# A gated recurrence followed by a bilinear feed-forward layer: a new order of the first steps, and nine more matmuls of zeros

## The chip, the core and the metric

The kernel runs on one core of one Trainium2 chip. The core has five engines that run their own queues in order and wait for each other by semaphores: TensorE (PE, with its weight loads shown as PEld), VectorE (DVE), ScalarE (ACT), GpSimd (POOL) and SyncE (SP), of which GpSimd and SyncE here also issue the DMAs that load and store. TensorE writes only to PSUM, eight banks of 512 words in each of 128 partitions; VectorE and ScalarE read the results from there. The metric is the time of one execution on the device in microseconds (us). The profile adds the span from the first to the last recorded instruction, and the granted clock of TensorE, as a share of full speed.

## The reference

Two computations, one after the other. The first is a recurrence for each of 4 batches x 8 heads, over 768 positions with heads of 48. A state of 48 x 48 decays by a vector and takes up an outer product at each position, and a query reads it:

```python
for t in range(S):
    state = alpha[:, :, t, :, None] * state + np.einsum('bhd,bhe->bhde', k[:, :, t], v[:, :, t])
    y[:, :, t] = np.einsum('bhd,bhde->bhe', q[:, :, t], state)
```

The second takes y as 3072 tokens of 384 features (the 8 heads side by side) and computes `(x @ w_a) * (x @ w_b) @ w_out`, with w_a and w_b of 384 x 1536 and w_out of 1536 x 384.

## The kernel before

The recurrence is worked in chunks. A block holds 256 positions of two batches, so there are six blocks, numbered 0 to 5 (blocks 0 and 1 are the first 256 positions of batches 0, 1 and of 2, 3). Within a block each batch (called u, 0 or 1) is split into two chunks of 128 positions, called g, and into two halves of four heads, called a and b or h = 0 and 1. Logs of alpha are summed along a chunk by matmuls with a triangular matrix. The exponentials of these sums scale queries and keys, so that a chunk becomes: scores (keys times queries), masked to the past, times the values; plus the queries times the state carried into the chunk; and a state that is passed on. The feed-forward layer then takes a block's 512 tokens, 128 of the 1536 hidden features at a time (12 groups f): an a product, a b product, their product to SBUF, and from these the output with w_out.

The order of all instructions is written by hand in the string PROGRAM. Each entry names a block and then its steps; each step issues the instructions of one small function, and every engine runs its own in that order. The scheduler adds only the waits. A step stands in the queues of the engines that it uses, so moving it past steps of other engines changes nothing on its own.

The steps that the change touches, with their arguments and the lines of what they issue:

- ld (L547), W (L527), Wo (L530): loads of alpha, k, q, v for a block, columns lo to hi of w_a or w_b, and rows of w_out. The last letter names the issuing queue, P for GpSimd, Y for SyncE. W and Wo are on GpSimd.
- ln (L554): log of alpha on ScalarE. B u half bank (L589, L590): its running sums, in float32, for block 0, straight from the two logs of a pair of rows. l2 (L562), H, L, A2 (L636): the same for block 1, by sums of pairs, split in two parts.
- E u i and E u b (L665): the exponentials, of the negated and of the plain sums (their tile carries the name prod in block 0). mk and mq (L676): keys and queries times them, on VectorE. lv (L650): a correction of k or q for half of the rows.
- dk (L698) and de (L719): sums of logs over a chunk by matmuls with two columns, and their exponentials, which decay the state.
- C u h bank (L736): eight transposes of scaled keys and queries, and Ce (L958 or L960): their copy to SBUF.
- v (L769, L771) and vs (L958, L960): copies of the values, straight and with rows crossed.
- K u g bank (L792) or K2 (L805): the product of keys and values; k (L819, L822, L823): the next state from it.
- D u h bank (L837): scores. M (L846): masked by VectorE. Mc and Mm (L850, L854): copied by ScalarE and then masked.
- SB, SA (L866): the carried part of the output of u. Y (L866): the part from the scores. X (L902, L904): that output to SBUF, as the input x of the layer.
- a f u bank, b f u bank (L921): the gate products of group f, for u = 0, 1 or both (written *), with 256 or 512 columns in three matmuls. as (L927): the a product to SBUF, in one of three copies. pr (L935): a times b, on VectorE.
- o m half bank (L943), ot (L958, L960), st (L976): outputs of 128 tokens, their copy and their store.
- fill n bank (L572): n matmuls of a 128 x 128 by a 128 x 512 tile of zeros into a PSUM bank. Nobody reads the result.
- cm, c1, ci, cu, cus, cz, cs, c2, c3: constants and zeroed tiles.

A bank's new writer waits until its last result has been read. In the order before, TensorE's queue starts with fill 7, B 0b, B 0a, dk 0, C 0 1, fill 2, C 0 0, D 0 1, K 0 0, D 0 0, SB 0, B 1a, B 1b, dk 1, Y 0, SA 0, C 1 0, K 1 0, C 1 1, K 1 1, D 1 0 and then the first gate products: a 1, a 2, b 1, a 3 of u = 0, D 1 1, SB 1, b 3, b 2, b 0, a 0, b 4.

The fill step, the gate products and the copy of the a product are these lines:

```python
    def fill(n, i):
        for _ in range(n):
            nc.tensor.matmul(bank(i), lhsT=wz[:, :C], rhs=wz, start=True, stop=True)

    def ff(ch, w, f, us, i):
        n = len(range(B)[us]) * C
        ch.pf["ab"[w], f, us.start, us.stop] = p = bank(i)[:, :n]
        for kk in range(KT):
            nc.tensor.matmul(p, lhsT=(wa_t, wb_t)[w][:, kk, f * 128:(f + 1) * 128], rhs=ch.xT[:, kk, us, :], start=(kk == 0), stop=(kk == KT - 1))
```

Of the kernel before, what the change touches and what calls it, by code (L numbers as in the profile page):

```python
# [34 lines left out]
0: as 0 0; b 4 0 5  # L35
1: ln 0; l2 0 P
0: Mm 1 1 V; SA 1; Y 1; K 0 1 6; pr 2 0; a 4 0 0; as 4 0; b 5 0 7; k 1 1 V; a 5 0 4; X 1 V; a 1 1 2
0: a 2 1 0
1: ld q 1 P
0: a 3 1 1; pr 0 0; pr 4 0; b 1 1 3; Wo 0 6; k 0 1 V; as 5 0; a 4 1 4; b 3 1 5; b 4 1 6; as 1 1; a 0 1 2  # L40
1: ln 1; l2 1 P
0: pr 1 1
1: ra 0; lv 0 q P; ld k 1 P
0: a 5 1 3; pr 5 0; as 3 1; b 0 1 1; Wo 6 12; as 4 1; b 2 1 4; pr 3 1; a 10 * 5
1: H 1 V; L 1 V
0: a 11 * 7; as 0 1; as 2 1; pr 2 1
# [24 lines left out]
0: a 9 * 5; as 9 *; b 8 * 0
1: C 0 1 7; mq 1 V; Ce 0 1 V; C 0 0 2
0: b 9 * 1; pr 9 *; o 2 0 3; as 8 *; pr 8 *
1: Ce 0 0 S; D 0 0 4; Mc 0 0; K2 0 0 2 6
0: o 0 0 7; o 3 0 0
1: k 0 0 V; k 0 1 V; SB 0 4
3: ld a * P
1: mk 1 V; D 0 1 1; M 0 1
0: o 3 1 -; ot 3 V; st 3 Y
1: v 0 S; vs 0 0 S; vs 0 1 S; Mm 0 0 V; C 1 1 6; Ce 1 1 V  # L80
2: ln *
0: o 0 1 -; ot 0 S
# [24 lines left out]
1: b 10 0 6; pr 10 0; a 6 0 7; as 7 0; b 7 0 1; pr 7 0; b 5 0 5; as 5 0
2: lv 1 k P
1: b 11 0 6; pr 5 0; SA 1
2: mq 0 V  # L110
1: Y 1
2: mq 1 V
1: b 6 0 1
2: mk 1 V; E 0 i
1: as 6 0; a 0 0 0; b 0 0 7; pr 6 0; a 11 0 4; X 1 S; a 2 1 5; b 3 0 2; as 0 0; pr 0 0; as 11 0; a 3 0 3
1: as 3 0; a 8 0 4; b 9 0 0; b 2 1 1; a 6 1 3; pr 11 0; as 2 1; a 9 0 5; as 9 0; pr 3 0; o 2 0 2
# [1061 lines left out]
```

## Time and profile before

| what | value |
|---|---|
| timed runs | 189.12, 189.28, 190.45 us (median 189.28) |
| profiled execution | 190.44 us |
| its span | 188.7 us |
| TensorE busy | 181.9 us, 96% of the span |
| VectorE, ScalarE, GpSimd busy | 152.6, 120.1, 53.6 us |
| bytes read and written | 25.98 and 4.74 MB |
| mean granted clock of TensorE | 0.991 |

Busy time is the time in which an engine had an instruction under way. Matmuls are pipelined, so the rows of TensorE overlap: the time that one takes of the queue is read from its start to the start of the next. A row of the timeline gives its start, the time to the end of its last instruction, the engine, the line in the kernel, the operation, what it writes and reads, and how many instructions it merges; in brackets stands the idle time before it and what ended that. The rows of stretches give, for each engine, its busy time and the number of its instructions, then the granted clock and the DMA engines' share and rate. Granted clock that isn't recorded at the start of a trace is shown as full.

### The profile page before, as it was taken

Reading aid. Unit: us, or ns where it says so; the run is one execution under the profiler, and the core shown is the slowest. Engines: PE = TensorE matmul, PEld = TensorE weight load, DVE = VectorE, ACT = ScalarE, POOL = GpSimd, SP = SyncE. Lnnn points to the kernel's source line nnn. Section 1 sums busy time; section 2 is a strip of 40 time slices with the busy share of each in tenths; the row PEclk is TensorE's granted clock in tenths of the full one; section 3 lists DMA queues with packets and bytes.
Section 4 is the critical chain, followed back from the end, with each engine's and each line's share of the span. In section 5 each row is a group of like instructions: output and inputs, shape, how many; then the busy total and the mean of one; then the engine's idle time right before and its main releaser. Section 6 shows DMA issues by size and latency. Waiting matters only on the chain.

```text
span 188.7 us, 6347 instructions
## 1 busy us (share of the span) xinstructions
PE 181.9 (96%) x2693; PEld 122.3 (65%) x2709; DVE 152.6 (81%) x271; ACT 120.1 (64%) x228; POOL 53.6 (28%) x74
## 2 busy tenths in 40 slices
PE   7979999999999999999999999999999999999993
PEld 3969886566778886754445644555457477565992
DVE  2484889788979799998889899999999945696862
ACT  4364865579995797797697949965980451526230
POOL 8999654998062240003500003300000000000000
PEclk9987999999999999999999999999999999999999
DMA  5999999999999899989999699939500102110053
GB/s 125 263 225 195 261 235 254 230 231 257 247 214 129 129 215 276 275 237 182 198 173 271 144 116 167 112 107 165 89 0 9 43 0 83 44 43 0 0 170 127
DMA packets 66285, 29.43 MB, mean 156 GB/s; under 512 B 55776, under 2 KB 64624, under 8 KB 66256
## 3 DMA queue, kind: packets, MB, share of 16 engines
q1 hardware_dynamic: 47488, 16.34, 41.2%
q0 software_dynamic: 18624, 12.58, 39.3%
q8 instruction: 21, 0.34, 0.7%
q10 hardware_dynamic: 144, 0.10, 0.2%
q14 instruction: 8, 0.07, 0.1%
HBM read 25.98 MB, written 4.74 MB: 163 GB/s over the span
## 4 chain that ended last, share of the span: by engine, by line
PE 90%; ACT 6%; issue 2%; DVE 1%
PE psum L921 47%; PE psum L943 12%; PE psum L1032 11%; PE psum L866 5%; PE psum L837 3%; PE psum L589 2%; PE psum L590 2%; PE psum L736 2%; PE psum L572 2%; ACT vx L958 2%; PE psum L631 1%; ACT la L554 1%; PE psum L792 1%; PE psum L805 1%; PE psum L698 1%
## 5 line engine op out<-in xcount | busy, mean ns | idle before, releaser
L921 PE MATMUL psum<-xT,wb_t 128*128 128x512 bf16 (+1 forms) x263 | 55.8, 336 | 0.5 <-issue 0.2
L921 PE MATMUL psum<-xT,wa_t 128*128 128x512 bf16 (+1 forms) x262 | 55.2, 335 | 0.5 <-issue 0.2
L921 PEld LDWEIGHTS <-wa_t 128*128 128x128 bf16 x270 | 25.7, 98 | 19.2 <-issue 0.5
L921 PEld LDWEIGHTS <-wb_t 128*128 128x128 bf16 x270 | 25.5, 98 | 18.4 <-issue 0.5
L943 PE MATMUL psum<-wo_t,prod 128*128 128x384 bf16 x144 | 26.1, 327 | 0.0
L958 ACT ACTIVATE ot<-psum 128x384 f32<-128x384 f32 (+1 forms) x23 | 11.2, 487 | 17.7 <-PE psum L1032 15.4
L650 POOL TENSOR_TENSOR q_t<-q_t,ra 128x384 f32<-128x384 f32 x6 | 6.4, 1072 | 53.6 <-ACT ra L643 31.1
L943 PEld LDWEIGHTS <-prod 128*128 128x128 bf16 x144 | 13.3, 98 | 8.3
L958 ACT ACTIVATE vx<-v_t 32x384 bf16<-32x384 bf16 x26 | 13.5, 521 | 1.5 <-DVE vx L771 1.1
L1032 PEld LDWEIGHTS <-prod 128*128 128x128 bf16 x144 | 12.0, 98 | 1.2
L850 ACT ACTIVATE m<-psum 128x768 bf16<-128x768 f32 x14 | 11.0, 810 | 2.3 <-PE psum L837 2.3
L676 DVE TENSOR_TENSOR QKp<-q_t,beta 128x768 bf16<-128x768 f32 x10 | 9.4, 952 | 1.9 <-ACT beta L665 1.6
L554 ACT ACTIVATE la<-a_t 128x1536 f32<-128x1536 f32 (+2 forms) x9 | 9.5, 1054 | 1.7 <-DMA a_t<-in_alpha_dram 1.5
L676 DVE TENSOR_TENSOR QKp<-k_t,invb 128x768 bf16<-128x768 f32 x10 | 10.1, 1013 | 0.3
L846 DVE TENSOR_TENSOR m<-psum,mask 128x768 bf16<-128x768 f32 x10 | 9.5, 949 | 0.6 <-PE psum L837 0.6
L1044 DVE TENSOR_TENSOR ot<-psum,ot 128x384 f32<-128x384 f32 x9 | 5.0, 555 | 5.9 <-issue 3.2
L866 PE MATMUL psum<-m,vx 64*64 64x128 bf16 (+1 forms) x576 | 8.7, 205 | 0.0
L547 POOL DMA_DIRECT2D v_t<-in_v_dram x8 | 8.5, 1064 | 0.0
L866 PE MATMUL psum<-kqT,Sm 64*64 64x128 bf16 x144 | 7.5, 220 | 0.4 <-DVE Sm L819 0.4
L866 PEld LDWEIGHTS <-vx 64*64 64x64 bf16 x576 | 7.6, 108 | 0.1
L854 DVE TENSOR_TENSOR m<-m,mask 128x768 bf16<-128x768 bf16 x14 | 7.4, 550 | 0.0
L665 ACT ACTIVATE prod<-psum 128x384 f32<-128x384 f32 x8 | 3.5, 488 | 6.0 <-PE psum L590 6.0
(292 smaller groups left out, 361.5 us busy)
## 6 DMA issues: line engine op xcount, KB each, us to landing
out_dram<-ot SPq DMA_DIRECT2D x23, 192.0 KB, 2.7
q_t<-in_q_dram SPq DMA_DIRECT2D x3, 768.0 KB
k_t<-in_k_dram SPq DMA_DIRECT2D x3, 768.0 KB
a_t<-in_alpha_dram POOLq DMA_DIRECT2D x2, 768.0 KB, 11.7
v_t<-in_v_dram POOLq DMA_DIRECT2D x4, 384.0 KB, 7.6
a_t<-in_alpha_dram SPq DMA_DIRECT2D x2, 768.0 KB
a_t<-in_alpha_dram POOLq DMA_DIRECT2D x3, 384.0 KB, 7.5
k_t<-in_k_dram POOLq DMA_DIRECT2D x3, 384.0 KB, 7.3
```

The lines of the kernel that those rows point to most:

```text
L547: eng.dma_start(out=t[:, us, hs].rearrange("p b h r d -> p (b h) (r d)"), in_=src[ch.b0 + us.start:ch.b0 + us.stop, hs, ch.s * 2 * C:(ch.s ...
L554: nc.scalar.activation(out=ch.la[:, us, hs].rearrange("p b h r d -> p (b h r d)"), in_=ch.a[:, us, hs].rearrange("p b h r d -> p (b h r d) ...
L650: eng.tensor_mul(x, x, by)
L676: eng.tensor_mul(QKp[ch.c % 2][:, u, j, :, hs, :D], src[:, u, hs].rearrange("p h r d -> p r h d"), f)
L846: nc.vector.tensor_mul(m, x, maskn())
L850: nc.scalar.activation(out=m, in_=x, func=AF.Copy)
L854: eng.tensor_mul(m, m, maskn())
L866: nc.tensor.matmul(o, lhsT=lhsT, rhs=rhs, start=(g, c) not in begun, stop=False, skip_group_check=True)
L921: nc.tensor.matmul(p, lhsT=(wa_t, wb_t)[w][:, kk, f * 128:(f + 1) * 128], rhs=ch.xT[:, kk, us, :], start=(kk == 0), stop=(kk == KT - 1))
L943: nc.tensor.matmul(op, lhsT=ch.prod[:, f, at:at + C], rhs=wo_t[:, f, :], start=(f == 0), stop=(f == NFF - 1))
L958: nc.scalar.activation(out=o_, in_=i_, func=AF.Copy)
L1032: nc.tensor.matmul(o[:, g], lhsT=A[:, f, g * C:(g + 1) * C], rhs=W[:, f], start=(not more and (apart or g == 0) and f == 0), stop=(f == LH ...
```

## The change

The steps of blocks 0 and 1, up to block 1's first gate products, are written in a new order, with other PSUM banks. The same steps are there, with the same arguments apart from the banks. The one step whose count differs is fill: 7 and 2 before, and 7, 5, 2, 1, 2, 1 after. TensorE's queue now starts with fill 7, B 0b, B 0a, C 0 1, dk 0, fill 5, K 0 0, C 0 0, D 0 1, fill 2, SB 0, D 0 0, fill 1, dk 1, B 1a, B 1b, fill 2, C 1 0, Y 0, SA 0, fill 1, C 1 1, D 1 0, K 1 0, a 3, a 2, K 1 1, D 1 1, SB 1, a 0, a 1, b 2, b 3, b 1, SA 1, K 0 1, Y 1. On VectorE, Ce 0 1 stands ahead of mk 0a and mq 0a, M 0 1 ahead of M 0 0, mq 1a ahead of mk 1a and mq 1b ahead of mk 1b; in block 1, mq 1 and mk 1 stand ahead of M 0 1. On ScalarE, de 0 and v 0 change places, ln 1 stands ahead of vs 0 0, and E 1a b ahead of E 1a i. From block 2's transposes on, the listing is the same. The first lines of the diff, cut:

```diff
-0: E 0b i; mk 0b V; ld k 1 P; ld q 1 P; cm 1; W b 0 256; cz 0 v P; E 0b b; mq 0b V; ld v 1 P; W a 256 768; dk 0 2
-0: C 0 1 3; E 0a i; mk 0a V; cz 1 q P; E 0a b; mq 0a V; v 0 S; Ce 0 1 V; fill 2 0; W a 0 256; de 0; W b 256 512
-0: C 0 0 1; Ce 0 0 V; D 0 1 2; K 0 0 0; vs 0 0 S; W b 512 768; cs 1 m P
-1: ld a 0 P
-0: D 0 0 4; k 0 0 V; SB 0 0; M 0 0; ln 1; B 1a 6
-1: ld a 1 P
-0: W a 768 1536; c2 P; W b 768 1536; E 1a i; E 1a b; B 1b 4
-1: ld q 0 P
-0: dk 1 6
-1: ld k 0 P
-0: vs 0 1 V; E 1b i; M 0 1; Y 0; mk 1a V; mq 1a V; mk 1b V; SA 0; E 1b b; mq 1b V; C 1 0 7; Ce 1 0 V
-0: K 1 0 2; C 1 1 3; de 1; k 1 0 V; Ce 1 1 V
-1: ld v 0 P
-0: K 1 1 4; X 0 S; v 1 S; vs 1 1 V; D 1 0 0; Mc 1 0; a 1 0 5; vs 1 0 V; as 1 0; a 2 0 2; b 1 0 3; as 2 0
-0: a 3 0 0; pr 1 0; as 3 0; D 1 1 6; SB 1 1; Mm 1 0 V; b 3 0 5; Mc 1 1; b 2 0 0; b 0 0 3; pr 3 0; a 0 0 6
+0: E 0b i; mk 0b V; ld k 1 P; ld q 1 P; cm 1; E 0b b; mq 0b V; E 0a i; E 0a b; C 0 1 7; Ce 0 1 V; dk 0 4
+0: mk 0a V; de 0; fill 5 0; W b 0 256; mq 0a V; K 0 0 6; k 0 0 V; C 0 0 7; Ce 0 0 V; v 0 S; ln 1; D 0 1 0
+0: M 0 1; fill 2 2; SB 0 2; D 0 0 4; fill 1 6; dk 1 6; M 0 0; vs 0 0 S; B 1a 0; E 1a b; vs 0 1 V; E 1a i; mq 1a V; B 1b 4
+0: E 1b i; E 1b b; mk 1a V; fill 2 7; C 1 0 7; mq 1b V; cz 0 v P; ld v 1 P; W a 256 768; cz 1 q P; W a 0 256; Y 0; SA 0
+0: mk 1b V; fill 1 0; C 1 1 0; v 1 S; Ce 1 0 V; D 1 0 4; Ce 1 1 V; X 0 S; W b 256 512; vs 1 0 V; de 1; K 1 0 7; k 1 0 V
+0: a 3 0 1; W b 512 768; cs 1 m P; Mc 1 0; Mm 1 0 V; as 3 0; a 2 0 6; K 1 1 0
+1: ld a 0 P
+0: as 2 0; vs 1 1 V; D 1 1 2; Mc 1 1; SB 1 3; a 0 0 5; as 0 0; Mm 1 1 V; a 1 0 1; b 2 0 6; b 3 0 2; pr 3 0
+0: as 1 0; b 1 0 5; SA 1; K 0 1 7; Y 1; k 1 1 V; a 5 0 0; b 0 0 1; a 4 0 2; pr 2 0; b 4 0 6; X 1 V
...
```

The rest of block 0's gate products and of block 1 (its sums A2, transposes C, scores D and states K2, the outputs o of block 0, and block 1's first gate products) follow in the same manner:

```diff
-0: a 5 1 3; pr 5 0; as 3 1; b 0 1 1; Wo 6 12; as 4 1; b 2 1 4; pr 3 1; a 10 * 5
...
-0: b 5 1 0; b 10 * 2
...
-0: pr 0 1; b 6 * 1
...
-1: H 0 V; L 0 V; lv 1 q P; A2 0 3; lv 1 k P
-0: a 8 * 6; pr 5 1; pr 10 *
...
-1: C 0 1 7; mq 1 V; Ce 0 1 V; C 0 0 2
+0: pr 0 0; b 5 0 3; as 5 0; b 3 1 4; a 5 1 0
...
+1: ld v 1 P; A2 0 5; H 1 V
...
+0: pr 0 1; a 11 * 4; a 10 * 6; as 2 1; b 2 1 7; pr 2 1
...
+0: a 7 * 2; as 7 *; as 4 1; b 4 1 0; b 10 * 1; pr 4 1
+1: dk * 7; A2 1 2
...
+1: mq 0 V; mk 0 V
+0: b 9 * 7
+1: v 0 S; E 1 i; C 0 0 2
```

More of the change, by code (lines that the diff above doesn't have):

```diff
@@ L108 @@
[L108 to L116, printed above, removed]
+0: cz 1 v P
+1: Mc 0 0; vs 0 0 S
+0: o 3 0 6; o 0 0 1
+1: M 0 1; SB 0 2; vs 0 1 S
+0: o 3 1 -
+1: C 1 0 4; C 1 1 5; k 0 1 V; Mm 0 0 V; Ce 1 0 S
+2: ln *
+0: ot 3 V; o 0 1 -
+1: Ce 1 1 V; v 1 V; vs 1 1 V
@@ new lines @@
+0: st 3 Y
+2: l2s 0 V
+1: D 1 1 6; Mc 1 1; SA 0
+2: l2s 1 V
+1: Y 0; X 0 S; vs 1 0 S
+2: l2 0 V
+0: ot 0 S
+1: K2 1 1 4 5; k 1 0 V
+2: R 0
+1: k 1 1 V
+0: o 2 1 -; c3 P
+3: ld a * P
+0: o 1 0 6; o 1 1 -
+1: a 2 0 2
+0: ot 1 S
+2: R 1
+1: a 4 0 7; a 5 0 1; as 2 0; b 2 0 4; D 1 0 5
+2: ra 1
+1: pr 2 0; as 4 0
+0: ot 2 S
+1: M 1 0
+2: AQ 2
+1: SB 1 6; as 5 0
+2: ra 0; E 0 i
+0: cs 1 0 P
+1: b 4 0 4; pr 4 0; a 1 0 0; as 1 0
+2: lv 1 q P
+1: Mm 1 1 V; b 5 0 1; a 10 0 5; a 7 0 4
+2: E 0 b
+1: as 10 0; b 7 0 0
@@ L120 @@
 2: lv 0 k V
-1: as 8 0; a 8 1 1; as 8 1; b 8 0 6; a 3 1 7; pr 9 0; a 10 1 0
+1: as 8 0; a 8 1 1; as 8 1; b 8 0 6; a 3 1 0; pr 9 0; a 10 1 7
 2: mk 0 V
```

105 lines of the change are left out of this document (45 added, 60 removed).

## The prediction

> **What bounds the kernel now.** I read the page's summary, its slices and the chain of work that ended last first.
>
> ```profile
> span 188.7 us, 6347 instructions
> ...
> PE 181.9 (96%) x2693; PEld 122.3 (65%) x2709; DVE 152.6 (81%) x271; ACT 120.1 (64%) x228; POOL 53.6 (28%) x74
> ...
> PEclk9987999999999999999999999999999999999999
> ...
> PE 90%; ACT 6%; issue 2%; DVE 1%
> ```
>
> TensorE is busy for 96% of the span and carries 90% of the chain, so TensorE's own queue sets the end. Times below count from the start of the span. The profiled execution took 190.44 us: 1.74 around a span of 188.70. The three timed runs were 189.12, 189.28 and 190.45, so the profile resembles the slowest of them, and that matters. The dip in the clock line is worth a table of stretches: busy time of each engine, then the granted clock.
>
> ```profile
> 9.25:12.66 3.41, 2.10 (x64) 1.64 (x64) 2.85 (x6) 2.97 (x6) 3.37 (x6) 1.00 1.05 245
> 12.67:16.08 3.41, 3.41 (x12) 3.41 (x13) 1.56 (x4) 0.74 (x2) 3.41 (x7) 0.51 1.54 190
> 16.08:19.49 3.41, 3.41 (x116) 2.97 (x114) 2.10 (x5) 2.04 (x7) 3.36 (x5) 0.99 1.40 204
> 20.68:65.00 44.32, 44.11 (x677) 32.43 (x676) 39.08 (x78) 33.25 (x69) 23.85 (x25) 1.00 1.16 219
> ```
>
> From 12.67 to 16.08 the clock is half; the 3.41 us before had TensorE busy for only 2.10. From 20.68 to 65.00 it idles for 0.21 of 44.32, so the middle cannot be shortened by reordering. A gain must come from before 20.68, where the gate products begin. TensorE's rows there (start, time to the last end, idle before):
>
> ```profile
> 1.19 3.17 PE L572 MATMUL psum<-wz 128*128 128x512 bf16 x7 [1.19 <-DVE og L472]
> ...
> 6.39 0.49 PE L589 MATMUL psum<-la,ut 128*128 128x192 f32 x2
> ...
> 7.79 0.91 PE L698 MATMUL psum<-og,la 128*48 128x2 f32 x32
> 8.62 0.62 PE L736 MATMUL psum<-ident,QKp 128*128 128x128 bf16 x8
> 9.08 0.38 PE L572 MATMUL psum<-wz 128*128 128x512 bf16 x1
> ...
> 10.58 0.34 PE L837 MATMUL psum<-kqT 64*64 64x128 bf16 x13 [0.46 <-ACT bl L719]
> ...
> 11.80 0.35 PE L866 MATMUL psum<-kqT,Sm 64*64 64x128 bf16 x6 [0.43 <-DVE Sm L819]
> 12.53 0.85 PE L589 MATMUL psum<-la,ut 128*128 128x192 f32 x2 [0.37 <-ACT la L554]
> ...
> 17.01 0.91 PE L698 MATMUL psum<-og,la 128*48 128x2 f32 x32
> 17.85 0.72 PE L866 MATMUL psum<-m,vx 64*64 64x128 bf16 x48
> 18.39 0.34 PE L866 MATMUL psum<-kqT,Sm 64*64 64x128 bf16 x6
> 18.67 0.62 PE L736 MATMUL psum<-ident,QKp 128*128 128x128 bf16 x8
> 19.22 0.43 PE L792 MATMUL psum<-v_t,QKp 64*64 64x48 bf16 x16
> 19.58 0.62 PE L736 MATMUL psum<-ident,QKp 128*128 128x128 bf16 x8
> ...
> 20.68 0.83 PE L921 MATMUL psum<-xT,wa_t 128*128 128x256 bf16 x6
> 21.34 0.49 PE L921 MATMUL psum<-xT,wb_t 128*128 128x256 bf16 x3
> ...
> 22.09 0.37 PE L837 MATMUL psum<-kqT 64*64 64x128 bf16 x16
> 22.29 0.34 PE L866 MATMUL psum<-kqT,Sm 64*64 64x128 bf16 x6
> ...
> 31.34 1.79 PE L921 MATMUL psum<-xT,wb_t 128*128 128x256 bf16 x9
> ```
>
> Three gaps (0.46, 0.43, 0.37) sum to 1.26 us. Then two running sums of logs (B 1a and B 1b) take 12.53 to 17.01, 4.48 us, where one like them (B 0a, 6.39 to 7.79) took 1.40 at full clock: 4.48 - 2.80 = 1.68 us lost to the clock. The seven leading fills took about 0.45 each (3.17 / 7), against 0.22 for 512 columns at full clock (six of 256 columns from 20.68 to 21.34), so the clock is low at the start too; the change doesn't touch that.
>
> What would this kernel take without that dip? Working B 1a from 12.53 at 1.40 and B 1b from 14.05 (it overwrites scores that the mask multiply of 13.09 reads until then, its row stands below), with the same work behind, the gates could begin at 19.0, 1.68 earlier. One price is to be paid back: the last slice of w_b is late (rows of GpSimd's issues, and of the loads with their KB and the us from issue to landing).
>
> ```profile
> 11.39 0.75 POOL L527 DMA_DIRECT2D wa_t<-in_moe_w_a_dram  x1
> ...
> 18.30 0.79 POOL L527 DMA_DIRECT2D wb_t<-in_moe_w_b_dram  x1
> ```
>
> ```profile
> wa_t<-in_moe_w_a_dram POOLq DMA_DIRECT2D x1, 384.0 KB, 6.6
> ...
> wb_t<-in_moe_w_b_dram POOLq DMA_DIRECT2D x1, 576.0 KB, 12.0
> ```
>
> It is issued at 18.30 and lands 12.0 later, at 30.3, and its first product (one half gate of 0.33 behind 31.34, so 31.67) would come at 30.0. So about 1.4 us would be left: 190.44 - 1.4 = 189.0, an estimate that falls beside the two quick timed runs. I read the three times as two executions without the dip and one with it.
>
> **The change, part by part.** The queues of GpSimd and SyncE keep their order exactly, DMAs included: only their places between other engines' steps differ in the listing. So the loads are issued and land as now, while GpSimd's few waits for ScalarE's logs move by less than the queues do. What changes is the order on TensorE, ScalarE and VectorE, PSUM banks, and nine more fills (18 for 9), 9 x 0.22 = 2.0 us of TensorE's time at full clock. The work of the three other engines is the same. Whether the fills cost depends on whether TensorE would have waited there, so I walk the queues. Durations from VectorE and ScalarE:
>
> ```profile
> 7.12 0.56 DVE L676 TENSOR_TENSOR QKp<-k_t,prod 128x384 bf16<-128x384 f32 x1 [3.09 <-ACT prod L665]
> 7.59 0.64 DVE L676 TENSOR_TENSOR QKp<-q_t,prod 128x384 bf16<-128x384 f32 x1
> ...
> 9.41 1.44 DVE L960 COPY kqT<-psum 128x1024 bf16<-128x1024 bf16 x2
> 11.30 0.36 DVE L819 TENSOR_TENSOR Sm<-psum,bl 128x192 bf16<-128x192 f32 x1 [0.45 <-PE psum L792]
> ...
> 13.09 0.96 DVE L846 TENSOR_TENSOR m<-psum,mask 128x768 bf16<-128x768 f32 x1
> ```
>
> ```profile
> 6.59 0.87 ACT L665 ACTIVATE prod<-psum 128x384 f32<-128x384 f32 x2 [1.86 <-PE psum L590]
> ...
> 9.44 0.84 ACT L769 ACTIVATE vx<-v_t 128x768 bf16<-128x768 bf16 x1 [0.68 <-DMA v_t<-in_v_dram]
> ...
> 11.63 0.84 ACT L554 ACTIVATE la<-a_t 128x768 f32<-128x768 f32 x1
> ...
> 18.77 0.81 ACT L902 ACTIVATE xT<-psum 128x768 bf16<-128x768 f32 x1 [0.46 <-PE psum L866]
> ```
>
> TensorE occupancy, start to next start: eight transposes 0.46, decay sums 0.84, a state product K 0.37, scores D 0.20, carried part S 0.28, inner part Y 0.54.
>
> Until B 0a ends (7.79) nothing moves. Now C 0 1 comes next instead of the decay sums; it waits for mq 0b, which ends at 8.23: a new gap of 0.5, in place of decay work. C 0 1 8.28 to 8.74, dk 0 to 9.58, fill 5 to 10.66. On VectorE, Ce 0 1 now stands ahead of mk 0a and mq 0a and waits for C 0 1: 8.92 to 9.6, then the two multiplies until 10.65. So K 0 0 could run at 10.2 and C 0 0 at 10.7: the five fills cost about 0.4 and hide the rest. K 0 0 10.66, C 0 0 11.03 to 11.49, D 0 1 to 11.69, fill 2 to 12.12 (k 0 0 done at 11.6), SB 0 to 12.39, D 0 0 (Ce 0 0 done at 12.37) to 12.6, fill 1 to 12.8, dk 1 to 13.66. The logs dk 1 needs are ready by 12.47 even if they start as late as now (11.63 + 0.84). B 1a follows at 13.66, since the mask multiply that frees its banks ends at 13.3; B 1b from 15.06 to 16.46. Against today that is 1.13 later for B 1a, but at full clock B 1b ends 0.55 earlier, with dk 1 already behind it.
>
> Next the chain through the other engines binds. E 1b i starts at about 16.6 (0.15 after the last matmul issues), E 1b b ends at 17.5; since mq 1b is now first and needs the second exponential, it runs 17.58 to 18.15, mk 1b to 18.65. Today's mk first would have gained some 0.4 here. Fill 2, C 1 0, Y 0, SA 0 and fill 1 lie inside this wait and cost nothing; without them TensorE would only stand. C 1 1 18.7, D 1 0 at 19.37 (Ce 1 0 stands behind mk 1b), K 1 0 to 19.95. There a 3 0 begins: its weights (issued 11.39, 6.6 to landing) are there at 18.0, and X 0, 0.81 after Y 0 and SA 0 end near 18.4, is out by 19.4. K 1 1 is still to do: 19.95 + 0.37 = 20.32 for what stands at 20.68 today. **Front: -0.4 us** (-1.2 if gates went as soon as X 0 is out; +0.4 if the new VectorE and ScalarE orders each slip by one multiply).
>
> Gates with the weights that land first: at 19.0 to 20.3 this saves a wait, but a 3 and a 2 would find their weights in either order, and today's a 1 waits for nothing at 20.68. Nothing is gained; the late w_b slice is now first used behind three wide a products and so costs nothing.
>
> From 20.3 on, TensorE has today's work and today has no gaps there, so changes of banks and order can only keep even or lose. Every gate step waits for the read of its bank four to six steps earlier, and only three copies of an a product may be alive. Walking the queues with half gates of 0.33 (21.34 to its successor), the tight places are b 5 0 behind X 1, a 10 behind pr 4 0, and block 1's C 0 0, which needs mk 0, now last of lv, pr, mq, mk on VectorE: some 0.25, more if GpSimd's concurrent multiplies stretch it. **Middle: +0.3 us, between 0 and +1.2.** The listing's tail is the same.
>
> **Sum:** 190.44 - 0.4 + 0.3 = 190.3 us against the profiled execution, and 1.0 above the median of 189.28, because the median has no dip to remove. The change buys with fills what lucky executions have for nothing.
>
> Of the clock, the row comes first: half clock behind a stretch whose longest gap is 0.46 us. The Trainium skill (TensorE: Matmul & The Clock Gate, Why this matters for your kernels) says to avoid idle gaps over some 3 us; the trace disagrees, as gaps of 0.46 summing to 1.26 sufficed. By that rule the gaps did not cause the dip, closing them does not remove it, and it stays: the last rival below.
>
> **Rivals.** *Front shorter (189.2).* The a step begins as X 0 comes out and the middle has no stalls: 190.44 - 1.2. For it: TensorE's added fills all lie in waits if the multiplies are quicker than here. Against: D 1 0 and K 1 0 stand ahead of a 3 in TensorE's queue.
>
> *The dip moves (191.9), the slower side.* From 16.5 to 19.9 TensorE now has fills 0.65, transposes, Y, S, D, K, and gaps near 0.5, without the sums that fill today's stretch 16.08 to 19.49. If that counts as idle, the next 3.41 us, all gates, go at half clock: 3.41 / 2 = 1.7, less 0.1 of stalls that it hides; 190.3 + 1.6. It decides once the granted clock falls after 19. The Trainium skill (TensorE: Matmul & The Clock Gate, Part 4: PE-mode transpose) says that transposes don't count as busy the way matmuls do, which speaks for it; no row here separates the two.
>
> *The gate order stalls (191.2).* Products wait on banks for the full 1.2: +0.9. For it: VectorE is busy for 39.08 of 44.32 us in the middle. Against: today's order under the same load doesn't stall.
>
> *The dip stays (191.5).* Fills of zeros don't keep the clock up, and the half clock takes 3.41 / 2 = 1.7 us from dk 1, B 1a and B 1b, of which the 0.5 that TensorE waits behind them hides a part: +1.2. Against: the leading fills are the same zeros, and full clock follows them.
>
> **How the numbers follow.** Forecast 0.52 (own range 189.7 to 190.9), front shorter 0.20, dip moves 0.12, gates stall 0.12, dip stays 0.04. Within 1% of 189.28 (187.4 to 191.2, about what a measurement of this kernel can tell from no change) lie the forecast, the shorter front, and half of the stalls: 0.78, less 0.03 kept for faster, so 0.75; slower 0.22; faster 0.03, since the front alone can't give 1.9 us and nothing else can gain. The range takes in -1.2 on one side and the moved dip on the other: 188.9 to 192.0.
>
> **What would show it.** Full clock from 6 to 20 us; B 1a starting near 13.7; the first gate product near 20.0; a gap near 8; and no row of TensorE with more than 0.3 us idle from 20 to 65. It is wrong if the granted clock drops anywhere after 6 us, if the first gate starts before 19.2 or after 20.8, or if gaps in the middle exceed 1.2 us.

## The result, and the profile after

| | before | after |
|---|---|---|
| median | 189.22 us | 195.69 us |
| lowest to highest of six runs | 188.79 to 190.45 | 195.02 to 196.07 |
| profiled execution, its span | 190.44, 188.7 | 195.82, 194.1 |

The ratio is 1.0333, 95% interval 1.0307 to 1.0359: slower, 3.7 us above the top of the range that was forecast. The page of the changed kernel has this:

```profile
span 194.1 us, 6359 instructions
...
PE 184.1 (95%) x2700; PEld 121.4 (63%) x2718; DVE 154.9 (80%) x271; ACT 120.0 (62%) x228; POOL 51.3 (26%) x74
...
PEclk9999999999999999999999999999999999999999
...
PE 81%; ACT 5%; issue 5%; DVE 4%; DMA 3%; DVEq 0%
```

The dip of the clock is gone, as forecast. TensorE's share of the chain fell from 90% to 81%, and "issue" rose from 2% to 5%: the span is longer by 5.4 us, TensorE's busy time by 2.2 us only. So TensorE stands more than before. Where, the table of stretches tells (after; stretches like those shown of before):

```profile
9.25:12.66 3.41, 3.36 (x71) 1.99 (x69) 2.45 (x6) 2.72 (x6) 3.37 (x6) 1.00 1.06 250
12.66:16.08 3.42, 3.17 (x66) 3.11 (x67) 2.39 (x4) 0.46 (x2) 3.42 (x6) 1.00 1.55 193
...
20.29:65.00 44.71, 41.16 (x657) 29.03 (x655) 37.95 (x71) 30.11 (x62) 21.68 (x23) 1.00 1.07 207
```

Up to 16 us there is full clock and hardly a gap: the front does what it was meant to. From the first gate product to 65 us TensorE is busy for 41.16 of 44.71 us, where it was busy for 44.11 of 44.32: 3.55 us idle instead of 0.21. The loss is in the middle. TensorE's rows there, with what ended the idle time:

```profile
14.26 0.59 PE L599 MATMUL psum<-la,ut 128*128 128x192 f32 x2
...
20.29 0.83 PE L931 MATMUL psum<-xT,wa_t 128*128 128x256 bf16 x6
...
24.57 0.24 PE L876 MATMUL psum<-kqT,Sm 64*64 64x128 bf16 x1 [0.42 <-issue]
...
41.10 1.07 PE L746 MATMUL psum<-ident,QKp 128*128 128x128 bf16 x16 [0.97 <-DVE QKp L686]
...
51.13 0.27 PE L876 MATMUL psum<-m,vx 64*64 64x128 bf16 x6 [0.35 <-issue]
...
60.96 0.49 PE L931 MATMUL psum<-xT,wb_t 128*128 128x256 bf16 x3 [1.59 <-DVE prod L945]
```

B 1a begins at 14.26 (13.66 forecast) and the first gate product, a 3, at 20.29 (19.95 forecast). Behind it stand two waits for VectorE, 0.97 us for QKp (block 1's mk 0, which C 0 0 transposes) and 1.59 us for prod (a gate multiply pr of block 1, whose bank the next b product writes), and two stalls that the profile calls "issue" (time in which the engine waited for nothing that the profile shows). VectorE and GpSimd at these two places, first VectorE of the changed kernel, then GpSimd:

```profile
37.37 0.72 DVE L945 TENSOR_TENSOR prod<-as__744,psum 128x512 bf16<-128x512 bf16 x1
37.99 1.38 DVE L686 TENSOR_TENSOR QKp<-q_t,beta 128x768 bf16<-128x768 f32 x1
39.29 1.75 DVE L686 TENSOR_TENSOR QKp<-k_t,invb 128x768 bf16<-128x768 f32 x1
...
57.85 2.71 DVE L864 TENSOR_TENSOR m<-m,mask 128x768 bf16<-128x768 bf16 x1
...
140.62 0.56 DVE L833 TENSOR_TENSOR Sm<-tmp,bl 128x384 bf16<-128x384 f32 x1 [0.94 <-DVE tmp L832]
```

```profile
37.50 1.05 POOL L660 TENSOR_TENSOR q_t<-q_t,ra 128x384 f32<-128x384 f32 x1
39.06 1.16 POOL L660 TENSOR_TENSOR k_t<-k_t,a_t 128x384 f32<-128x384 f32 x1 [0.52 <-DMA k_t<-in_k_dram]
...
55.99 1.01 POOL L660 TENSOR_TENSOR q_t<-q_t,ra 128x384 f32<-128x384 f32 x1 [10.90 <-ACT ra L653]
58.16 1.01 POOL L660 TENSOR_TENSOR q_t<-q_t,ra 128x384 f32<-128x384 f32 x1
59.14 0.99 POOL L660 TENSOR_TENSOR k_t<-k_t,a_t 128x384 f32<-128x384 f32 x1
```

The same instructions of the kernel before, on VectorE and on GpSimd:

```profile
35.62 1.57 DVE L676 TENSOR_TENSOR QKp<-k_t,invb 128x768 bf16<-128x768 f32 x1
...
54.42 0.55 DVE L854 TENSOR_TENSOR m<-m,mask 128x768 bf16<-128x768 bf16 x1
...
135.03 0.56 DVE L823 TENSOR_TENSOR Sm<-tmp,bl 128x384 bf16<-128x384 f32 x1
```

```profile
39.17 1.76 POOL L650 TENSOR_TENSOR k_t<-k_t,a_t 128x384 f32<-128x384 f32 x1
...
53.42 1.01 POOL L650 TENSOR_TENSOR q_t<-q_t,ra 128x384 f32<-128x384 f32 x1 [7.04 <-ACT ra L643]
55.58 1.02 POOL L650 TENSOR_TENSOR q_t<-q_t,ra 128x384 f32<-128x384 f32 x1
```

Block 1's Mm 1 1, a multiply of two SBUF tiles, takes 0.55 us at 54.42 in the kernel before: it falls between two multiplies of GpSimd (53.42 to 54.43 and from 55.58). In the changed kernel the same instruction begins at 57.85, 0.31 us ahead of GpSimd's multiplies at 58.16 and 59.14, ends behind both, and takes 2.71 us. What stands behind it on VectorE, the gate multiplies pr, comes 2 us late, and TensorE waits for a bank. Likewise mq 0 and mk 0 of block 1 take 1.38 and 1.75 us beside GpSimd's multiplies at 37.50 and 39.06; alone they take 0.94 to 0.96 (rows below). The gate multiply at 37.37, with one input in PSUM, takes its 0.72 beside GpSimd as elsewhere.

Positions of two of TensorE's steps that both kernels have sort the loss. From the first gate (with K 1 1's 0.37 us added in the changed kernel, where it still has to run: 20.29 + 0.37 = 20.66) to the first state product K2 of block 2 it is 66.48 - 20.68 = 45.80 us before and 70.80 - 20.66 = 50.14 after: +4.34. From there to TensorE's last end, 185.46 - 66.48 = 118.98 before and 190.83 - 70.80 = 120.03 after: +1.05, though the listing of that part is the same. The front gives 20.66 - 20.68 = 0.0 against the profiled execution with its dip. The sum is 5.4, and 190.44 + 5.4 = 195.8.

In one series of timed runs of before, the five at clock 1.0 took 188.60 to 189.60 us (median 188.72), and the two at 0.991 took 190.79 and 190.81: the dip costs 2.1 us there, and 1.9 in three other series. No run of the changed kernel has it. So the change costs 6.4 to 7.0 us against undisturbed runs of before (medians of 188.72 to 189.30 by series), and a part of that must be a later front, which the comparison with the dipped profile hides.

### The profile page after: what moved, and what is told of

Read it like the earlier page. It is cut to its first block, busy times and chain, and to the rows that moved or that the text cites. A ratio compares the mean times of both kernels' runs of the same rounds, so it can differ in the third digit from the quotient of the medians.

```text
span 194.1 us, 6359 instructions
## 1 busy us (share of the span) xinstructions
PE 184.1 (95%) x2700; PEld 121.4 (63%) x2718; DVE 154.9 (80%) x271; ACT 120.0 (62%) x228; POOL 51.3 (26%) x74
## 4 chain that ended last, share of the span: by engine, by line
PE 81%; ACT 5%; issue 5%; DVE 4%; DMA 3%; DVEq 0%
PE psum L931 39%; PE psum L953 11%; PE psum L1042 11%; PE psum L876 6%; DMA kqT<-QKp 3%; PE psum L847 3%; PE psum L582 3%; PE psum L746 2%; DVE QKp L686 2%; PE psum L708 1%; PE psum L641 1%; PE psum L599 1%; ACT vx L968 1%; PE psum L802 1%; PE psum L815 1%
## 5 line engine op out<-in xcount | busy, mean ns | idle before, releaser
L686 DVE TENSOR_TENSOR QKp<-q_t,beta 128x768 bf16<-128x768 f32 x10 | 9.9, 995 | 1.0 <-ACT beta L675 0.8
L864 DVE TENSOR_TENSOR m<-m,mask 128x768 bf16<-128x768 bf16 x14 | 9.5, 704 | 0.0
L876 PEld LDWEIGHTS <-Sm 64*64 64x64 bf16 x144 | 5.1, 106 | 3.7 <-issue 2.8
```

The costliest lines, as they stand in the source:

```text
L686: eng.tensor_mul(QKp[ch.c % 2][:, u, j, :, hs, :D], src[:, u, hs].rearrange("p h r d -> p r h d"), f)
L864: eng.tensor_mul(m, m, maskn())
L876: nc.tensor.matmul(o, lhsT=lhsT, rhs=rhs, start=(g, c) not in begun, stop=False, skip_group_check=True)
```

## The experiments

The theories at the start: the new order of the rest costs the time, by VectorE's multiplies that meet GpSimd's (theory); or the new front costs it, by nine more fills and a later start of what follows (rival).

**Old front, new rest, and the reverse.** In the first kernel the steps up to the first gate product are those of before (D 1 0 in bank 4, and K 1 1 behind the first gates, as in the changed kernel), and the rest is that of the changed kernel. In the second it is the other way round (C 1 1 and one fill in bank 6, where they overwrite the sums of dk 1 before de 1 reads them: block 0's second batch gets other decays; the work is the same).

```diff
 # old front, new rest
-D 1 0 0
+D 1 0 4
 ...
 # new front, old rest
-fill 1 0; C 1 1 0; ... D 1 0 4
+fill 1 6; C 1 1 6; ... D 1 0 0
```

> The old order up to D 1 0 and X 0 (with D 1 0 in bank 4), then the new order of everything behind. If the loss lies in the middle, the 4.3 us that accrue from 20.7 to 66 us and the 1.1 behind come along: 193.5 to 195. If the front costs most, 189.5 to 191.

> The new order up to K 1 0 and the first gate product (fills included), then the old order of everything behind (C 1 1 in bank 6, D 1 0 in bank 0 and K 1 1 in bank 4, so that the old gate steps find their banks free). If the loss lies in the middle, where TensorE's rows of the changed kernel show gaps of 0.6 to 1.8 us, this runs at 189.2 plus the about 1.3 us by which the new front is later than the old one without the clock dip: 190 to 191. If the new front with its nine more fills costs most of the 6.5 us, it is at 193 or above.

Measured: old front with new rest 193.02 us (191.03 to 195.43, the longest of the four with a clock of 0.991), ratio 1.0156 (1.0057 to 1.0255). New front with old rest 192.18 us (191.82 to 192.81), ratio 1.0151 (1.0079 to 1.0223). Neither theory has it alone: by their medians the halves cost 4.3 and 3.4 us over the 188.75 of before in that series. The profiled run of the first is its shortest, 191.03 us; TensorE's row of its first gate product and of the wait, then VectorE's mk 0 and Mm 1 1:

```profile
18.34 0.83 PE L931 MATMUL psum<-xT,wa_t 128*128 128x256 bf16 x6
...
56.95 0.49 PE L931 MATMUL psum<-xT,wb_t 128*128 128x256 bf16 x3 [1.58 <-DVE prod L945]
```

```profile
36.44 0.94 DVE L686 TENSOR_TENSOR QKp<-k_t,invb 128x768 bf16<-128x768 f32 x1
...
53.85 2.69 DVE L864 TENSOR_TENSOR m<-m,mask 128x768 bf16<-128x768 bf16 x1
```

This front had no dip and starts the gates at 18.34, with K 1 1's 0.37 us still to come: 18.71 on the scale of before. That is the measure that the prediction lacked (it had estimated 19.0): the new front is 20.66 - 18.71 = 1.95 us later than this undisturbed old one. With the 4.34 of the middle and the 1.05 behind it that makes 7.3, a little over the 6.4 to 7.0 that the change costs. Mm 1 1 takes 2.69 us here too, so the new order of the rest brings it, whatever the front; mk 0 takes 0.94, as it begins 0.34 us ahead of GpSimd's multiply (36.78). In the second kernel the first gate begins at 20.73, with K 1 1 done: 2.0 us later than 18.71. Its middle is 0.7 us longer than before's, and 0.8 us more is lost in the tail, of which below.

**Mm 1 1 ahead of the collision.** One step of block 1 moves up on VectorE's queue in the changed kernel.

```diff
-1: pr 2 0; as 4 0
+1: Mm 1 1 V; pr 2 0; as 4 0
...
-1: Mm 1 1 V; b 5 0 1; a 10 0 5; a 7 0 4
+1: b 5 0 1; a 10 0 5; a 7 0 4
```

> The changed kernel with one instruction moved on VectorE: block 1's mask multiply Mm 1 1 stands ahead of pr 2 and M 1 0, when GpSimd still waits, instead of behind pr 4, when GpSimd multiplies block 2's queries and keys. If a VectorE instruction with two inputs in SBUF stands still while GpSimd works on SBUF, Mm 1 1 takes 0.55 us instead of 2.71, TensorE's gap of 1.6 us near 59 is gone, and the time is 194.0 to 194.4. If the 2.71 us have another cause that belongs to this instruction, it is as long in the new place and the time stays at 195.7. If VectorE was not what TensorE waited for, Mm 1 1 is short and the time stays.

Measured: 193.98 us (193.00 to 194.31), ratio 1.0233 (1.0143 to 1.0323): 1.7 us below the changed kernel, as expected. VectorE's row of it:

```profile
55.25 0.55 DVE L864 TENSOR_TENSOR m<-m,mask 128x768 bf16<-128x768 bf16 x1
```

The same instruction on the same tiles, 2.6 us earlier and clear of GpSimd, takes 0.55 instead of 2.71 us, and TensorE's wait of 1.59 is gone. This settles the first cause.

**mq 0 and mk 0 of block 1 earlier.** The correction lv 0 k and the two multiplies move up by a few gate multiplies.

```diff
-0: ... b 10 * 1; pr 4 1
+0: ... b 10 * 1
+1: lv 0 k V
+0: pr 4 1
+1: mq 0 V
...
-0: b 7 * 3; as 10 *; pr 7 *; a 9 * 0
-1: E 0 i; lv 0 k V
-0: pr 10 *
+0: b 7 * 3; as 10 *; a 9 * 0
+1: E 0 i; mk 0 V
+0: pr 7 *; pr 10 *
...
-1: mq 0 V; mk 0 V
```

> The changed kernel with block 1's lv 0 k, mq 0 and mk 0 moved up on VectorE, ahead of pr 4 1 and pr 7, into the time in which it idles (33.6 to 36.3 us) and GpSimd issues DMAs but does not multiply. If the stretched multiplies (1.38 and 1.75 us for 0.95) delay block 1's transposes, TensorE's gap of 1.0 us near 40 goes and the time is 194.4 to 194.9. If GpSimd's issuing of DMAs stretches them as much as its multiplies do, mk 0 still takes 1.5 us or more, but ends earlier, and most of the gap still goes. If TensorE makes up for that gap anyhow, 195.7.

Measured: 194.99 us (194.70 to 195.61), ratio 1.0300 (1.0227 to 1.0373): 0.7 us less than the changed kernel, a little short of what was expected (0.8 to 1.3). TensorE's row of C 0 0 and VectorE's of mk 0:

```profile
39.88 1.06 PE L748 MATMUL psum<-ident,QKp 128*128 128x128 bf16 x16
```

```profile
34.85 1.75 DVE L688 TENSOR_TENSOR QKp<-k_t,invb 128x768 bf16<-128x768 f32 x1
```

The wait of 0.97 us ahead of C 0 0 is gone, but mk 0 still takes 1.75 us: here it lies beside DMA issues of GpSimd (from 34.83 on), and GpSimd multiplies only from 36.87. In before's profile its 1.57 us at 35.62 lie beside such issues too; but mq 0 at 33.98 in this kernel takes 0.95 beside the issue from 33.68. Something stretches the multiplies there sometimes; that it is the issues is not shown.

**Both moves.**

> The changed kernel with both moves on VectorE's queue together: Mm 1 1 ahead of the wait for GpSimd's block-2 multiplies, and block 1's lv k, mq and mk of batch 0 earlier. Theory of two separate collisions with GpSimd: the two gains add, 195.7 - 1.7 - 0.7 = 193.3 us, and TensorE shows neither the wait on prod near 59 us nor the one on QKp near 40 us. Rival, that what is saved at the first place is lost again at the second (one chain of the gates paces both): 194.0 us, that is the better of the two alone.

Measured: 192.93 us (191.89 to 193.83), ratio 1.0222 to before's 189.29 in that series (1.0169 to 1.0274): 2.8 below the changed kernel, of which 0.5 in the profiled run lies before the first gate product (19.77 instead of 20.29). All four runs are below the rival's 194.0: by the times the gains add. But the moves don't bring the middle back. It is still 48.29 - 0.37 - 45.80 = 2.1 us longer than before's in this profile, with both waits gone; 1.27 us of that are two "issue" stalls (0.73 and 0.54).

**Old front and both moves; old front and Mm 1 1 alone.**

> The old front with the new rest (as in the run with the old front), and both moves on VectorE's queue. Theory of the two collisions with GpSimd as the price of the new rest: 193.0 - 1.7 - 0.7 - (up to 0.4, as both together gave 2.8 on the changed kernel) = 190.2 to 190.6 us in the median, with a part of the runs 2 us higher where the clock drops. Rival, that the new order of the gates itself costs something beside the collisions: 191.2 us or more.

> The old front with the new rest, and only Mm 1 1 moved ahead of the wait for GpSimd's block-2 multiplies; mq and mk of block 1 stay where the changed kernel has them. With the old front they don't meet GpSimd's multiplies (TensorE had no wait there in the run with the old front). Theory, that Mm 1 1's collision is the whole price of the new rest beside the front: 191.0 (the undisturbed profile with the old front) - 1.7 = 189.2 to 189.6 us where the clock holds, about that of the kernel before. Rival, that the new rest costs something more: 190.3 us or more, as with both moves.

Measured: with both 190.52 us (189.82 to 190.97, ten runs), ratio 1.0051 (1.0025 to 1.0077); with Mm 1 1 alone 191.92 us (189.59 to 193.21), ratio 1.0110 (1.0032 to 1.0189). The first is what the theory gave, and yet 1.1 us above before's 189.40 in that series: some of the price of the new rest is in neither collision. Its profile has a new wait of TensorE, 0.79 us at 36.26, for a gate multiply that now stands behind the moved multiplies, and an "issue" stall of 0.52. The second is by its median what the rival gave. The one execution of it with a trace shows the other collision instead. VectorE's mq 0 and mk 0 in it, then GpSimd:

```profile
37.36 0.96 DVE L686 TENSOR_TENSOR QKp<-q_t,beta 128x768 bf16<-128x768 f32 x1
38.22 2.73 DVE L686 TENSOR_TENSOR QKp<-k_t,invb 128x768 bf16<-128x768 f32 x1
```

```profile
37.38 1.79 POOL L660 TENSOR_TENSOR q_t<-q_t,ra 128x384 f32<-128x384 f32 x1
39.15 0.98 POOL L660 TENSOR_TENSOR k_t<-k_t,a_t 128x384 f32<-128x384 f32 x1
```

In this execution, the slowest of the six, the two meet after all, and worse (2.73 us, and TensorE waits 1.50 us for QKp); in the profiled run with the old front they had just missed each other. Its front is also 1.1 us later (first gate at 19.43), and one "issue" stall takes 1.07 us. The one run of 189.59 us fits the expected time without the collision; neither it nor the four near 191.9 has a trace, so what makes the median is not shown. GpSimd's multiply of q begins at 36.78, 37.38, 37.50 and 38.01 us in four of these kernels, whose first gates begin anywhere from 18.34 to 20.68: it moves by 1.2 us where they move by 2.3, since it follows its own queue of DMA issues. VectorE's place against it is a matter of tenths of a microsecond. The new order puts mk 0 at the edge.

**Fewer and shorter fills.** The changed kernel has eleven fills behind the first seven (two in before; where the expectations say "added", they mean all eleven). Three kernels: none of the eleven; six of them; eleven of 128 columns instead of 512.

```diff
-de 0; fill 5 0; W ...  M 0 1; fill 2 2; SB ...  fill 1 6; dk ...  fill 2 7; C ...  fill 1 0; C
 # none
+de 0; W ...  M 0 1; SB ...  dk ...  C ...  C
 # six
+de 0; fill 2 0; W ...  M 0 1; fill 1 2; SB ...  fill 1 6; dk ...  fill 1 7; C ...  fill 1 0; C
 # eleven short ones
+de 0; warm 5 0; W ...  M 0 1; warm 2 2; SB ...  warm 1 6; dk ...  warm 2 7; C ...  warm 1 0; C
```

> The changed kernel without the 11 added idle matmuls behind the first 7. Theory A: the fills only lengthen the front and move the place of an instruction fetch in the tail, so without them the front is 0.4 to 1.0 us shorter and the stall of block 5's state multiply (0.94 us of wait for the decay load) is gone too: 194.0 to 194.6 us. Theory B: the fills keep TensorE's granted clock at full speed, so without them the clock drops to half for some 3.4 us as in the profile of before, and the time is 195.7 us or more, up to 197.5.

> The changed kernel with 6 of its 11 added idle matmuls (5 become 2, 2 become 1 twice; the two single ones stay). Each takes 0.21 us at full clock. Theory, that most of the added idle work lies on TensorE's path and not in gaps, and that fewer suffice to keep the clock: no run with the clock down, the first gate step about 1 us earlier, 194.5 to 194.9 us, less another 0.5 to 1 us if the state multiply's wait for block 5's decay load goes as well. Rival, that all 11 are needed: the clock drops as it did without any, 195.5 to 197 us.

> The changed kernel with its 11 added idle matmuls of 512 columns each replaced by one of 128 columns (0.06 us in place of 0.21 us). Theory, that the front is 2 us later than before's by the idle work alone: the first gate step at 18.6 us instead of 20.3 us if the clock holds; how much of that is left at the end depends on whether block 1's mk 0 then meets GpSimd's multiplies (0.5 us more with 6 fills). 194.2 to 195.2 us. Rival, that the order costs it: first gate step at 19.5 us or later with the clock at full speed, 195 to 195.7 us; or the short ones don't hold the clock, and it is 195.9 us as without any.

Measured: none 195.91 us (194.02 to 197.18, ratio 1.0348, 1.0268 to 1.0429); six 195.83 us (195.39 to 199.43, ratio 1.0330, 1.0299 to 1.0362); short ones 195.14 us (194.52 to 195.87, ratio 1.0285, 1.0209 to 1.0360), inside the expected 194.2 to 195.2. Without any, all four runs have a granted clock of 0.982 to 0.991. Its stretches, with the clock behind POOL's column:

```profile
8.00:12.00 4.00, 3.06 (x100) 2.52 (x100) 3.27 (x6) 2.61 (x7) 3.89 (x8) 1.00 1.12 274
12.00:16.00 4.00, 4.00 (x41) 3.98 (x42) 1.80 (x4) 0.98 (x2) 4.00 (x7) 0.53 1.50 198
16.00:20.00 4.00, 4.00 (x71) 3.72 (x69) 1.53 (x3) 2.17 (x5) 3.45 (x6) 0.61 1.38 233
```

0.94 us of idle time in the first 4, no gap over 0.5, and then the clock averages 0.53 and 0.61 for 8 us, longer than in before. With all eleven it held in all six runs, with short ones in all four, with six in three of four (the fourth took 199.43 us at 0.974; the kernel before had one such run as well, 195.80 at 0.974). So in this order the fills do hold the clock, and the rival that they don't is out; by the medians they cost what they bring.

How much idle time brings a dip the runs don't say. In the profile with the old front and Mm 1 1 alone moved TensorE is busy for only 2.05 of the 3.42 us from 8.68 to 12.10, less than ahead of before's dip, and the clock stays at 1.00; and before itself dips in some of its runs only. TensorE's first gate product and C 0 0 with six, VectorE's mk 0 there, and the first gate product with short ones:

```profile
19.42 0.83 PE L931 MATMUL psum<-xT,wa_t 128*128 128x256 bf16 x6
...
40.63 1.07 PE L746 MATMUL psum<-ident,QKp 128*128 128x128 bf16 x16 [1.49 <-DVE QKp L686]
```

```profile
37.85 2.72 DVE L686 TENSOR_TENSOR QKp<-k_t,invb 128x768 bf16<-128x768 f32 x1
```

```profile
18.95 0.83 PE L931 MATMUL psum<-xT,wa_t 128*128 128x256 bf16 x6
```

The first gate comes 0.87 us earlier with five fewer (five of 0.21 are 1.05) and 1.34 us earlier with short ones (eleven times 0.15 are 1.7). So some four fifths of the idle work lies on TensorE's path and not in gaps, and of the 1.95 us by which the new front is late, at least 1.3 are fills. The expectation for the end was still wrong with six: what the front gained, the middle took back. GpSimd hardly moved, so VectorE met it at a worse point, mk 0 took 2.72 us, and the wait at C 0 0 grew from 0.97 to 1.49 us.

**The tail.** The listing of the last part is the same, and yet it takes 1.05 us more. In the changed kernel the multiply `Sm<-tmp,bl` of block 5 waits 0.94 us (VectorE's row at 140.62, above; no wait at 135.03 in before), and TensorE's SA behind it. The row names tmp as what ended the wait, but tmp was done at 139.67. Its other operand bl is the decay of block 5, which two DMAs of SyncE load in pieces of 4 bytes. The trace's records of DMA packets show, beside the data, 21 packets of 16 KB per execution on an instruction queue (fetches), each 0.9 to 1.8 us long. In us, from the span's start:

| kernel | second issue of bl | fetch | last packet of bl | issue to last packet |
|---|---|---|---|---|
| before | 132.28 | 135.43 to 136.31 | 135.08 | 2.80 |
| old front, new rest | 132.59 | 135.57 to 136.52 | 135.38 | 2.79 |
| old front, both moves | 132.10 | 134.71 to 135.70 | 134.97 | 2.87 |
| changed, no fills | 138.02 | 140.97 to 141.95 | 140.83 | 2.81 |
| changed | 136.96 | 138.21 to 139.34 | 140.38 | 3.42 |
| changed, Mm 1 1 moved | 134.87 | 136.45 to 137.33 | 138.37 | 3.50 |
| new front, old rest | 133.03 | 134.67 to 135.60 | 136.63 | 3.60 |
| changed, short fills | 135.54 | 137.21 to 138.14 | 139.17 | 3.63 |

Where a fetch falls into the middle of the load, the load takes 0.6 to 0.8 us longer. The other profiles agree. Of all sixteen, eight have a fetch in the middle of this load, which takes 3.39 to 3.67 us there, and 2.74 to 2.90 in the rest; and the tail, from block 2's K2 to TensorE's last end, takes 119.8 to 120.4 us in the eight and 119.0 to 119.5 in the rest. The eight are just the kernels with four to nine more idle matmuls than before. The account of this is that the fills shift the stream, as nine more of them are 18 more instructions for TensorE (a fill is a weight load and a matmul), so each later fetch comes earlier against the work. To try that alone, the kernel before got nine short idle matmuls in the gaps of its front:

```diff
-Ce 0 0 V; D 0 1 2; ... k 0 0 V; SB 0 0; M 0 0; ln 1; B 1a 6
+Ce 0 0 V; warm 3 7; D 0 1 2; ... k 0 0 V; warm 3 7; SB 0 0; M 0 0; ln 1; warm 3 7; B 1a 6
```

> The kernel before with 9 idle matmuls of 128 columns added in three places where TensorE waits in the front (18 instructions more on TensorE, about 0.1 us of work at each place). Theory, that the place of an instruction fetch in the stream decides the stall in the tail: the fetch by block 5 falls into the decay load as in the changed kernel, the state multiply L823 waits about 1 us for bl, and the time is 188.7 + 0.9 = 189.6 us. Rival, that the stall belongs to the new order of the tail: no such wait, 188.6 to 188.9 us. In no run does the clock drop if short idle work in those gaps is enough.

Measured: 190.14 us (189.34 to 190.79, nine runs), ratio 1.0051 (1.0020 to 1.0081) to before's 189.29 in that series: 0.85 more, for 0.9 expected. Its row on VectorE, and its stretches:

```profile
134.62 0.56 DVE L823 TENSOR_TENSOR Sm<-tmp,bl 128x384 bf16<-128x384 f32 x1 [1.17 <-issue]
```

```profile
9.25:12.66 3.41, 2.89 (x74) 2.28 (x74) 2.93 (x6) 2.96 (x6) 3.37 (x6) 1.00 1.08 244
12.67:16.08 3.41, 3.41 (x56) 3.17 (x58) 2.56 (x6) 1.70 (x4) 3.41 (x6) 1.00 1.52 188
```

With the old order of everything, the multiply now waits 1.17 us; the load took 3.58 us from its second issue at 130.78, with a fetch from 132.07 to 133.32 in it. So the new order is not needed for it; some more instructions ahead of it suffice. And the clock held in all nine runs, with 0.52 us idle in the stretch where before idled for 1.31; as most runs of before keep it too, nine runs don't show that the short matmuls did that.

**A better front for the kernel before.** Three kernels: de 0 and ln 1 earlier on ScalarE's queue; with that, the first gates in the order a 2, a 3, a 1, b 1; or instead the first loads of w_a swapped and b 1 ahead of a 2.

```diff
 # all three
-v 0 S; Ce 0 1 V; fill 2 0; W a 0 256; de 0; ... vs 0 0 S; ... M 0 0; ln 1; B 1a 6
+de 0; v 0 S; Ce 0 1 V; fill 2 0; W a 0 256; ... ln 1; vs 0 0 S; ... M 0 0; B 1a 6
 # second
-a 1 0 5; vs 1 0 V; as 1 0; a 2 0 2; b 1 0 3; as 2 0; a 3 0 0; pr 1 0; as 3 0
+a 2 0 5; vs 1 0 V; as 2 0; a 3 0 2; as 3 0; a 1 0 3; as 1 0; b 1 0 0; pr 1 0
 # third
-W a 256 768; ... W a 0 256; ... a 2 0 2; b 1 0 3; as 2 0
+W a 0 256; ... W a 256 768; ... b 1 0 3; a 2 0 2; as 2 0
```

> The kernel before with two steps moved on ScalarE's queue alone: de 0 ahead of v 0, and ln 1 ahead of vs 0 0. In before's trace K 1's matmuls waited 0.46 us for bl (de 0) and B 1a 0.37 us for la (ln 1). Theory, that these waits both delay the front and let the clock drop in some runs: no run at half clock, gaps at 10.1 and 12.2 us gone or below 0.2, 188.0 to 188.4 us. Rival, that the front is paced by VectorE behind them: 188.6 to 188.9 us, some runs near 190.8 still.

> The kernel before with de 0 and ln 1 earlier on ScalarE's queue, and its first gate steps in the order a 2, a 3, a 1, b 1. In the run with the two ScalarE moves alone, TensorE waited 0.96 us at 18.1 us for the weights of a 1, while those of a 2 and a 3 were issued earlier. Theory, that the weights then bound the start of the gates: the wait shrinks to 0.3 us or less, 188.2 to 188.5 us, no run at half clock. Rival, that those of a 2 land as late as those of a 1 (the transfers share their engines): the same 188.9 us.

> The kernel before with de 0 and ln 1 earlier on ScalarE's queue, the two first loads of the a weights in the other order (the 256 columns of a 0 and a 1 ahead of the next 512), and b 1 ahead of a 2. Theory, that the order of landing bounds the start of the gates: a 1 starts without a wait near 18.1 us, 188.0 to 188.5 us. Rival: a 2 then waits as a 1 did, 0.3 us later in all, 188.6 to 188.9 us.

Measured: 188.95 us (ratio 1.0014, 0.9987 to 1.0040; one of its ten runs took 196.77 at a clock of 0.974), 189.34 us (0.9997, 0.9961 to 1.0033) and 189.13 us (0.9978, 0.9953 to 1.0004). None is distinguishable from before. The first still waits for its weights:

```profile
19.05 0.83 PE L921 MATMUL psum<-xT,wa_t 128*128 128x256 bf16 x6 [0.96 <-DMA wa_t<-in_moe_w_a_dram]
```

The third removes that wait (first gate at 18.54, and TensorE's gaps over 0.06 us come to 0.57 in all its profile, 1.58 in before's), and one of its twelve runs has the dip, against two of twelve of the second and five of 29 of before. The old front without a dip begins the gates at 18.71 as it is (18.34 with K 1 1 to come). What these edits could give beyond 0.2 us is a rarer dip; these counts don't show one, and a median would hardly show it. No kernel of these runs is measurably faster than before.

## Why the prediction was wrong

- **What bounds the kernel; the dip; the reading of three times.** Right in kind: a run without the dip is 1.9 to 2.1 us shorter, and the change removes the dip. Mis-sized: 1.4 was forecast. Undisturbed gates were estimated at 19.0 (the walk itself, with B 1b from 14.05, gives 1.56 us saved and 19.12); they begin at 18.71, and at 18.91 and 19.80 in two other profiles with the old front. That the gaps of before "sufficed" is too strong: a profile with more idle time kept the clock. The sum started from 190.44 and is not touched by this; its comparison with the median is, as undisturbed runs have medians of 188.7 to 189.3.
- **Front: -0.4.** Measured 0.0 (20.66 for 20.32 forecast), inside its bounds of -1.2 to +0.4. B 1a came 0.6 late. The first five fills were to cost about 0.4 and the last three nothing; by the shorter fills, at least 1.3 us of all eleven lie on the path. That the term still came within 0.4 is luck in part: it was taken against a front with the dip, and against the undisturbed one of 18.71 the new front is 1.95 us later.
- **Middle: +0.3, between 0 and +1.2. This is the step that failed:** it measured +4.34. Its walk named block 1's C 0 0 behind mk 0 and priced it at "some 0.25, more if GpSimd's concurrent multiplies stretch it"; 0.97 was idle there. Mm 1 1 was not walked against GpSimd at all, and cost 1.7. That such a meeting is dear stood in the profile of before, in GpSimd's multiply of k that took 1.76 at 39.17 for 1.0, beside VectorE's mq 1 at 39.15; the prediction did not use this row. The rest, 4.34 - 0.97 - 1.7 = 1.7 us, is not settled: 0.77 of it is the two "issue" stalls ahead of 24.57 and 51.13, and for the remaining 0.9 TensorE is busy longer with the same work.
- **"The listing's tail is the same."** True and not enough: +1.05 us, the step between the profiles with a fetch in block 5's decay load and those without. No row of before could have told the size; that the fills are instructions, too, which have to be fetched, could have been thought of.
- **Gates with the weights that land first: nothing gained.** Agrees so far as tried: the two other orders in the kernel before made no difference that could be measured.
- **The rivals.** "The gate order stalls" (191.2) had the right place and a third of the price. "The dip moves" and "the dip stays" are out: the clock is 1.00 from 6 us on. "Front shorter" is out. What was to show the forecast wrong did: gaps in the middle over 1.2 us.

Of the collision the Trainium skill (GPSIMD Engine Reference, 8. Key points) says that GpSimd shares its SBUF interfaces with VectorE and contends with VectorE instructions that have two SBUF inputs. The trace agrees, 2.71 us for 0.55, and the gate multiplies, with one input in PSUM, were not stretched (0.72 us beside GpSimd or not). That section gives no price; the runs do, below.

Of the clock, the Trainium skill (TensorE: Matmul & The Clock Gate, Why this matters for your kernels) warns of idle gaps over some 3 us. The runs disagree, as the prediction said: without fills the clock dropped in all four runs, with no gap over 0.5 us ahead of it in the profile (0.94 us idle in 4), and eleven matmuls of 128 columns in those places held it in four of four. But a sum of gaps is no rule either, as the profile with 2.05 of 3.42 us busy shows.

## What to carry to other kernels

Before a multiply of two SBUF tiles is moved on VectorE's queue, look at what GpSimd does at its new place, and cost a meeting at the whole of GpSimd's multiplies that are left, not at a few tenths; then see who stands behind it on VectorE. Fill gaps of TensorE with as little idle work as holds the clock (a quarter of the columns did here), since what exceeds the gap is on the path. And compare a change with the undisturbed runs of the kernel before, not with the one execution that was profiled.

## What the runs showed of the hardware

**VectorE and GpSimd exclude each other whole.** Where one of them multiplies two SBUF tiles and the other begins such a multiply, the second ends as if it had done next to nothing until the first had ended. Mm 1 1: GpSimd ends at 60.13 (59.14 + 0.99), and the multiply at 60.56, 0.43 later, for 0.55 alone. mq 0 in the changed kernel: GpSimd ends at 38.55, mq 0 at 39.37, 0.82 later, for 0.94 to 0.96 alone; mk 0: 40.22 and 41.04, 0.82. With Mm 1 1 alone moved (old front): 40.13 and 40.95, 0.82, after two multiplies of GpSimd in a row, which let nothing in between them. It goes the other way as well: GpSimd's multiply at 37.38 there takes 1.79 instead of 0.99 us, and ends 0.85 after VectorE's mq 0 (38.32). So a collision costs the later one whatever is left of the earlier, up to 2.2 us here. Who counts as the later is open for Mm 1 1: by its row it begins 0.31 us ahead of GpSimd's multiply, in the last 0.3 us of a DMA issue of GpSimd (56.96 to 58.15), and is held by both multiplies in all six profiles with it at this place; with the old front and both moves it begins 0.29 ahead of one, with no issue beside it, takes 0.55, and GpSimd is the one stretched (1.14).

**A load in small pieces takes longer with an instruction fetch in its middle.** A fetch of 16 KB inside the load of 4-byte pieces goes with 0.5 to 0.9 us more for it: eight of sixteen profiles have one there, and those are the eight with the longer load. TensorE also stalls with no cause in the profile ("issue"), for 0.16 us in before's profile and up to 1.07 us in that of the old front with Mm 1 1 moved, in stretches of many short matmuls; in the changed kernel a fetch begins 2.2 us before each of the two. In all sixteen profiles 19 of the 21 such stalls of 0.2 us or more end 2.3 to 2.8 us after a fetch begins. That fetches cause these stalls was not tried and stays open.
